# A clamp with its two bounds swapped, steps moved between engines, and a new order of all steps, in an attention and gated projection kernel

## The chip, the cores and the metric

The kernel runs on one core of one Trainium2 chip. The metric is the device time of one execution in microseconds. The core's engines are TensorE (PE, matrix multiplication into PSUM), VectorE (DVE), ScalarE (ACT), GpSimd (POOL, which does not touch PSUM in this program) and SyncE (SP), from which all of this kernel's transfers are issued. Each engine works through its own instructions in order; semaphores tie them together.

## What is computed

The first stage is attention between a sequence `x` of 512 positions and a state of 32 rows, for 8 batches of 8 heads of 64 channels, read both ways. The second stage multiplies a gate, which is a causal five-tap convolution over positions behind a sigmoid, with a matrix product, and projects the result.

```python
def _attn_ref(x, state):            # x: 8,8,512,64   state: 8,8,32,64
    scale = 1.0 / np.sqrt(D)
    scores = scale * np.matmul(x, state.transpose(0, 1, 3, 2))
    a = softmax(scores)             # over the 32 state rows
    xread = np.matmul(a, state)
    a2 = softmax(scale * np.matmul(state, x.transpose(0, 1, 3, 2)))   # over the 512 positions
    sread = np.matmul(a2, x)
    return np.concatenate([xread, sread], axis=2)

def _moe_ref(x, w_val, conv_w, w_out):   # x: 8,544,512, heads side by side
    gate_pre = sum over k of conv_w[k] * x shifted by 4 - k positions
    gate = 1.0 / (1.0 + np.exp(-gate_pre))
    return (gate * (x @ w_val)) @ w_out
```

The weights reach the kernel as 64-bit integer arrays that hold float32 pairs; the kernel reads them as two 32-bit words, shifted by 16 bits, and joins a float from the two.

## The kernel before

**Steps and order.** The program first makes a list of 1,200 numbered steps, each a small function that issues one to a few instructions. The string `ORDER` (line 33) then lists the steps to issue, one number each; a letter behind a number gives the engine to a step that several could do: `a` ACT, `v` DVE, `g` POOL. Steps without a letter have a fixed engine. Nothing else decides the order: each engine gets its instructions in the order of the list. `SLOTS` gives every tile its buffer, in the order in which the tiles are first used. Steps that no list names are left out; among the 1,200 are 60 `warm_up` steps (two small matmuls each, on PE, whose result nobody reads), of which the order before uses 11.

**Weights.** `w_val` and `w_out` come in four parts each (w_val parts are called v0 to v3, w_out parts o0 to o3), the convolution weights in one (conv). For each part: `load_words` (SP), `words_top` (ACT: the top 16 bits to float, tile wc), `words_bound` twice (lines 270 to 274: wc clamped to a range of large negative or of large positive numbers, tiles ws0 and ws1), `words_sum` (POOL: ws0 + ws1 into wc, line 227), `words_int` (ACT: to integer, tile wt in PSUM, line 282), `words_join` (DVE: joined with the low bits, line 287). A w_out part is then split into `woh` (`high`, a copy to a rounded type) and `wol` (`low`, the rest, line 227).

**Batches.** For each batch b: transposes of x or `x_blocks_T` on DVE; `scores`; the softmax over positions (`max_s`, `exp_s`) and the one over state rows (`max_n`, `sub_n`, `exp_n`, `sum_n`, `scale_n`, `probs`, tiles sl and ex, 128x1024); `ah` and `al`, high and low part of the result; `exp_T`, `state_read`; `state_val` (line 343: state times all four joined w_val parts, tile sgv); `read`, which makes xr; per 128 channels `gate_first`, `gate_tap` three times, `gate_last`, `gate_add` (line 227), `gate`; `values` (line 538), `gated` (tile g), its parts `gh` (`high`) and `gl` (`low`); then per 128 positions `project` (lines 547 to 549), a copy out of PSUM (`project_copy`, tile o) and `store`. Batch 0 makes its gate with `tap_state` (POOL) and `read_conv` (PE). A tail does the same for the 32 state positions of all batches (`tail_taps`, `tgh`, `tgl`, `tail_project`, `tail_copy`, `tail_store`).

**Around the start.** The order before has POOL do, from the first w_val clamp on: both clamps and the sum of v0, two clears, the sums of v1 and v3 (whose clamps DVE does), a clamp of v2, `tap_state`, `scale_n` of batch 0, the other clamp of v2, both of o1, `sub_n` of batch 1, the sum of v2, both clamps of o0, the sums of o1 and o0, `scale_n` of batch 1, then the first `wol`. On PE, `exp_T` of batch 2 stands ahead of `state_val(0)`.

Of the kernel before, what the change touches and what calls it, by code (L numbers as in the profile page):

```python
# [14 lines left out]
ALU = mybir.AluOpType  # L15
# [18 lines left out]
52 98 10 107 97 110 95 207 210 96 72 24 197 53 198 105 11 111a 196 13v 112a 12g 19 211a 109a 103 14g 195 15 106a 16  # L34
212v 108v 94 99 104v 209a 22 20 100v 101 17 1179 102a 1197 117 73 31 23a 74v 208a 113 21a 75v 18 119 76g 25 45 203 114
325 335a 1168 120 38 205 115 26g 204a 27g 118 323 201 206a 28g 121 202a 324 199 116 322 1177 456 334 200a 122v 458 337
32 213 34v 46 468 33v 217 29 48v 47v 123 65 128 214 35g 130 218 77 332 336a 124 49g 39 460 129a 54a 58 40g 78 333a
140g 461 330 131a 215 328 331a 127 194 326 219 216 125g 132 221 471 329a 1176 133 459 327a 30 66 454 340 41g 455 338a
126 36 68g 230 134 67g 453 339a 50 342 135 1196 222g 344 469 136a 341 220 51 231a 1178 1153 232 59 345 42g 141 90a 229
457 223 61g 37 463 233a 60g 464 224 43 55 69g 343 346 62g 70 714 44 347 79 71 225g 63 359 462 148 137 145 64 600 151  # L40
234 465 356 91g 226 470 138a 56 466 139a 235 57a 348 244 227a 472 154 236 228g 252 467 585 588 142 254 586 245 321 473
255 360a 349g 155 597 253a 158 601 478 86a 584 156a 256 602 603 479 475 157g 595 166 80 587 159 598 266 247 82g 596
267a 582 257g 474 357 160a 167 162 358a 477 161g 476 589 350 81g 248 489 87g 88a 239 163 490a 351 237 361 89g 238a
240a 362 242a 146 170 241 352g 449 363 249 171 452 258 448 243 147a 259 279 268 592 149 273 168a 83g 591 280 261 150a
246a 491 269 250g 152 274 84 262 275 492a 281 153a 85 164a 169g 291 270 92a 498 251 353 271g 182 501a 276 183 165g
499a 502 277a 292 500 272 293 93g 282 260a 184 263 371 278g 480 185 379 264g 285 294 393 286 381 283a 143 172 395 354a
284g 287 144v 604 188 186a 382 723 265 481g 173 593 380a 288 590 189 725 174a 383 176 450 713 396 482 384g 177 599
295a 366 483 729 372 296g 728 190 175 369a 451 191 289a 374 355g 722 367a 364 724 178 370 187 365a 394a 368 179 385
375 309 386 484g 397 303 192a 388 180a 412 594 387a 413 398g 376 406 733 727 605 485 730 290g 580 304 389 486a 583 310
607 732 734 311 390 608 735 312 373a 391g 606 407 313a 609 414 377g 392 610 503 612 408 518 305 415 613g 512a 306 736  # L50
378 520 315 399 409 307a 316 487g 521 611 308 317 855 504 522 856 538 511 715 731 418 614 318 513 719 717 419 506 519a
314 420 514 720 410a 523g 493 718 319a 726 297 615 864 411g 524 494 193 298 867 525 848 400 488 616g 527 495 539 416a
401 421 505a 402 721 299 422a 528 849 532 423g 976 515 300 507 866 737 516g 854 301a 403 581 181 508 621 404a 845 533
517 739 865 405g 544 622a 850 742 534 741 545 509g 550 529 743 442 617 526a 417g 443 510 740 546 535 530g 444 547 536a
551 738 548a 635 537v 531 618a 868 549g 552 540 744 860 657 445 852 619g 636 844 659 430 859 541 658a 431 861 638 446a
846 436 857 553 745g 637a 862 437 660 851 554a 438 447 643 661 320 630 712 555g 645 639 432 633a 662g 646 433 746 634
424 434a 747 425 663 542a 623 439 631a 640 543g 644a 426 853 440a 670 641g 863 650 992 762 435 632 716 748g 858 496
671 497a 765a 620 427 652 763a 676 647 624a 672 428a 653 648g 753 869 764 754a 654 649 626 766 682 873 625 673 664 980
627 665 871 977 651a 574 870 993 642 983 683 752 872 989 874 575 981 674v 875 994 684 749 675g 986 576 984 991 577 876
750a 988 655g 987 562 982 578v 677 302 751g 656 685 678 755 686a 679 568 756a 990 767 687g 985 997 847 563 884 978 789  # L60
877g 569 579 768 791 996 564 999 770 790a 441 565 998 782 792 666 566a 628 995 570 878 793 556 680a 784 794g 557 769a
667 558 668v 795 571 771 757 669v 572a 758 772 783a 573 559 629a 785 775 773g 796 560a 777 885 561 797 1000 886a 429
798 759 567 786 887 979 802 879 787g 888a 760 1001 774 761v 803 880g 1006 890 889 1002 688 1005 891 681g 799 804 776a
894 1003 1007 800v 1004 1019 778 814 895a 881 808 815 779 816 882a 809 896 780g 689 897a 817 690 898 801g 781 810 1008
788 899 811 1009g 691 900 694 692v 921 695 1112v 1020a 812a 923 696 915a 902 700 914 903 706 1114a 924 701 813v 922a
697 916 702 698a 925 707 805 926g 708 904 709 917 901a 1026 818v 710a 883v 711 1017 1027a 928 806v 1018a 819v 826 1010
1028 905g 703 918 1110a 940 807v 1029a 929 906 946 1030 1113g 704a 827 1011 927 705 832 907 693 930 947 1012g 931 934
909 833 941 1111g 1013 935 1022 908v 919g 834 910 820 1016 920 942 821 943 822 911 944a 1021 912v 823 932v 933v 892
835 1023 893v 824a 1014v 828 913 825 945v 948 836a 1031 1015g 949 837 950a 1066 1032 936 829 1033a 937 1115g 1039 838
1034 1046 1067 1041 1108a 1024 839 1035 1025a 938a 1060 1042 830a 939g 1061 1036 831 840 1048 952 1037v 958 1043 1038  # L70
953 1049 1040a 841 1053 1050 1044g 1129 1072 1055 959 1109v 1047a 954 842v 1128 1062 1051v 843 1073 1056 1119 970 1118
1121 1052 964 1074 965 1116v 960 951v 966 1063 955 1117v 1068 967 1064v 1075 1124 968a 1076v 1065v 969 1120 1123 1134
1057 1077g 1122 1045 1054v 1078 1125 1090 956v 971 1069 957 1079 1070v 1133 1058v 1071v 1059 1126v 961 1130 972 1102
1127v 973 1131 1096 1103 1097 1132 1080 1135 1084 1081 1138 1136v 1085 1137v 1098 1082v 962v 1139 1083v 1104 974v 1099
975 699 1091 1144 1086 1105 1092 1106a 1100a 1140 1107 1101 1093 1141 1094v 1087 1095 1142v 963 1145 1143 1088v 1146
1147 1089 1198 1148a 1189 1190 1149
""".split()

SLOTS = dict(
    ps=  # L80
    "01234567312412756372456713631762631570754713564260431250413761561573613561762762412650774032230574617205347043"
    "17067124035760631577620165314203674175204127601657231762052643542760341043726651042602365702146",
    x="0120122102",
    sT="01",
    xT="01230123012301230123012301230123",
    xq="01201202102201010122",
    e2="0121021202102012",
    e2T="0120120210201202",
# [4 lines left out]
    swh="0100100101",  # L93
    swl="011011010",
# [19 lines left out]
def state_attention_gated_kernel(  # L114
# [155 lines left out]
    def words_bound(e, word, side, *key):  # L270
        p, n = word()[..., 0].shape
# [530 lines left out]
```

## Time and profile before

| | |
|---|---|
| time, median of 3 runs | 249.15 us (248.99 to 249.51) |
| the profiled execution, its own time | 247.34 us |
| its span in the trace | 245.6 us |
| PE busy | 224.2 us (91%) |
| DVE busy | 199.6 us (81%) |
| ACT busy | 151.4 us (62%) |
| POOL busy | 146.9 us (60%) |
| moved by DMA | 33.04 MB, 135 GB/s on average |

Busy time is the time in which at least one instruction of the engine runs; since matmuls overlap, a busy PE is not PE at its peak. In the rows below PEld is the load of weights into PE, PEclk the granted clock of PE as a share of full speed, `<-` ahead of a name what a wait ended with, and L227 a line of the kernel (a helper's, for all copies and differences: there the tile tells which step it is).

### The profile page before, as it was taken

How to read it: one execution, taken by the hardware profiler on the slowest of the kernel's cores; microseconds unless marked ns; L12 is line 12 of the kernel's file. 1: busy time of each engine (PE TensorE's matmuls, PEld its weight loads, DVE VectorE, ACT ScalarE, POOL GpSimd, SP SyncE). 2: the span in 40 equal slices, each digit the busy share in tenths (PEclk: the TensorE clock that was granted, in tenths of full speed). 3: DMA queues.
4: the chain of work that ended last, by engine and by line, in shares of the span. 5: the costliest groups of instructions: out<-in, count | busy, mean ns of one | idle time of the engine just before them, and what ended most of it. 6: DMA issues, size and time to landing. Idle time of an engine off the chain costs nothing.

```text
span 245.6 us, 4958 instructions
## 1 busy us (share of the span) xinstructions
PE 224.2 (91%) x1847; PEld 156.7 (64%) x1847; DVE 199.6 (81%) x320; ACT 151.4 (62%) x320; POOL 146.9 (60%) x109
## 2 busy tenths in 40 slices
PE   1986894799899999999999999999999999979994
PEld 1764661345466666767665766666677678868783
DVE  0489964759979999989999959998998699998730
ACT  2588754789677978967987658676581666011010
POOL 3278999769998996778867492545276432200000
PEclk9999799589999999999999999999999999999999
DMA  4899936256300764577373578600021211110046
GB/s 128 298 378 303 245 96 179 83 155 173 112 31 0 235 205 119 169 235 220 86 213 107 146 212 254 216 3 0 4 89 41 88 44 43 45 40 3 35 160 189
DMA packets 23029, 33.04 MB, mean 135 GB/s; under 512 B 6858, under 2 KB 15070, under 8 KB 23006
## 3 DMA queue, kind: packets, MB, share of 16 engines
q1 hardware_dynamic: 23006, 32.73, 43.5%
q8 instruction: 14, 0.23, 0.4%
q14 instruction: 9, 0.07, 0.1%
HBM read 23.81 MB, written 8.91 MB: 133 GB/s over the span
## 4 chain that ended last, share of the span: by engine, by line
PE 62%; DVE 18%; POOL 8%; DMA 4%; ACT 2%; issue 2%; SPq 1%; DVEq 0%; ACTq 0%; POOLq 0%
PE val L538 15%; PE op L547 9%; PE op L548 9%; PE op L549 8%; PE sgv L343 4%; DVE tacc L573 4%; DVE acc L518 3%; POOL ws_o L273 3%; PE srp L424 3%; PE xr L478 3%; PE e2p L415 2%; PE sc L378 2%; DVE ws_v L273 2%; DMA x<-x 2%; POOL ws_v L273 2%
## 5 line engine op out<-in xcount | busy, mean ns | idle before, releaser
L518 DVE SCALAR_TENSOR_TENSOR acc<-xr,cw,acc 128x511 f32<-128x511 f32 (+2 forms) x84 | 59.3, 735 | 3.2 <-ACT xt L514 2.7
L547 PE MATMUL op<-woh,gh 128*128 128x512 f32 x128 | 52.7, 412 | 1.8 <-DVE last L224 1.6
L548 PE MATMUL op<-wol,gh 128*128 128x512 f32 x128 | 50.6, 396 | 0.9 <-POOL wol L227 0.9
L549 PE MATMUL op<-woh,gl 128*128 128x512 f32 x128 | 50.4, 394 | 0.0
L227 POOL TENSOR_TENSOR acc<-acc,last 128x508 f32<-128x508 f32 x24 | 32.8, 1367 | 25.1 <-DVE acc L518 17.9
L227 POOL TENSOR_TENSOR gl<-g,gh 128x512 fp32r<-128x512 f32 x21 | 27.9, 1327 | 20.6 <-DVE gh L216 13.7
L547 PEld LDWEIGHTS op<-woh,gh 128*128 128x128 f32 x128 | 24.0, 188 | 14.1 <-issue 5.8
L548 PEld LDWEIGHTS op<-wol,gh 128*128 128x128 f32 x128 | 24.1, 188 | 6.2 <-POOL wol L227 1.7
L549 PEld LDWEIGHTS op<-woh,gl 128*128 128x128 f32 x128 | 24.0, 188 | 5.6
L543 DVE SCALAR_TENSOR_TENSOR g<-sig,val 128x512 f32<-128x512 f32 x32 | 21.6, 678 | 4.6 <-PE val L538 3.4
L530 ACT ACTIVATE sig<-acc 128x512 f32<-128x512 f32 x28 | 17.5, 633 | 11.7 <-POOL acc L227 6.6
L214 ACT COPY o<-op 128x512 f32<-128x512 f32 x24 | 14.1, 596 | 14.9 <-PE op L549 14.7
L513 ACT ACTIVATE acc<-xr,cw 128x512 f32<-128x512 f32 x28 | 19.1, 697 | 5.4 <-PE xr L478 5.3
L222 ACT ACTIVATE last<-xr,cw 128x508 f32<-128x508 f32 x26 | 18.0, 693 | 3.9 <-POOL acc L227 2.1
L227 POOL TENSOR_TENSOR al<-sl,ah 128x1024 fp32r<-128x1024 f32 x6 | 14.7, 2452 | 8.8 <-DVE ah L216 5.1
L538 PE MATMUL val<-ah,swh 128*128 128x512 f32 x56 | 18.0, 408 | 0.0
L538 PE MATMUL val<-al,swh 128*128 128x512 f32 x56 | 17.7, 402 | 0.0
L538 PE MATMUL val<-ah,swl 128*128 128x512 f32 x56 | 17.5, 398 | 0.0
L415 PEld LDWEIGHTS e2p<-ident,e 128*128 128x128 f32 x64 | 9.6, 207 | 11.1 <-ACT e L408 7.6
L227 POOL TENSOR_TENSOR ex<-ex,rc 128x1024 f32<-128x1024 f32 x8 | 15.4, 1920 | 1.6 <-DVE rc L464 1.5
L368 DVE STREAM_TRANSPOSE xT<-xq 128x512 f32<-128x512 f32 x20 | 13.8, 700 | 2.9 <-DMA xq<-x 2.9
L214 ACT CAST gh<-g 128x512 fp32r<-128x512 f32 x22 | 13.8, 631 | 3.6 <-DVE g L543 3.6
(131 smaller groups left out, 461.9 us busy)
## 6 DMA issues: line engine op xcount, KB each, us to landing
xq<-x SPq DMA_DIRECT2D x80, 124.0 KB, 3.6
x<-x SPq DMA_DIRECT2D x32, 256.0 KB, 5.3
out<-o SPq DMA_DIRECT2D x32, 256.0 KB, 2.3
ow<-w_out SPq DMA_DIRECT2D x4, 511.8 KB, 8.3
vw<-w_val SPq DMA_DIRECT2D x4, 511.8 KB
sg<-state SPq DMA_DIRECT2D x8, 64.0 KB, 3.3
z<-state SPq DMA_DIRECT2D x16, 32.0 KB
out<-to SPq DMA_DIRECT2D x8, 64.0 KB, 1.7
```

The lines of the kernel that those rows point to most:

```text
L214: nc.scalar.copy(out, in_)
L222: nc.scalar.mul(out, in_, factor)
L227: (nc.vector if e == "DVE" else nc.gpsimd).tensor_tensor(out, a, b, op=how)
L273: (nc.vector if e == "DVE" else nc.gpsimd).tensor_scalar(get(f"ws{side}", *key)[:p, :n], get("wc", *key)[:p, :n], least, most, op0=ALU.max ...
L513: nc.scalar.mul(get("acc", b, pr), pt, cw[:, HALO, pr:pr + 1])
L518: nc.vector.scalar_tensor_tensor(acc[:, d:], get("xr", b, pr)[:, :S - d], cw[:, HALO - d, pr:pr + 1], acc[:, d:], op0=ALU.mult, op1=ALU.add)
L530: nc.scalar.activation(get("sig", b, pr), get("acc", b, pr), AF.Tanh, scale=0.5)
L538: nc.tensor.matmul(get("val", b, k), w[:, g, c], a[:, g], start=(term == 0 and g == 0), stop=(term == terms - 1 and g == NG - 1))
L543: nc.vector.scalar_tensor_tensor(get("g", b, k), get("sig", b, k), 1.0, get("val", b, k), op0=ALU.add, op1=ALU.mult)
L547: nc.tensor.matmul(pt, gh, woh[:, k], start=(k == 0), stop=False)
L548: nc.tensor.matmul(pt, gh, wol[:, k], start=False, stop=False)
L549: nc.tensor.matmul(pt, gl, woh[:, k], start=False, stop=(k == NPR - 1))
```

## The change

Three things change. `words_bound` takes the minimum first and the maximum second, with the same two bounds. The order is a new one for all steps. In it, steps that several engines can do are given out anew:

| step | before | after |
|---|---|---|
| clamps of the words | 11 POOL, 7 DVE | 18 POOL |
| `gl`, `al`, `wvl`, `tgl`, the tail's low part (differences of two SBUF tiles) | POOL 30, DVE 16 | POOL 46 |
| `gate_add` | 24 POOL, 4 DVE | 28 POOL |
| `sub_n` | 7 POOL, 1 DVE | 8 POOL |
| `gh` | 22 ACT, 10 DVE | 32 ACT |
| `ah`, `wvh`, `tgh`, the tail's high part | 9 ACT, 5 DVE | 14 ACT |
| `exp_T_copy` (e2T) | 16 ACT | 13 ACT, 3 DVE |
| `project_copy` (o) | 24 ACT, 8 DVE | 21 ACT, 11 DVE |
| `state_val_high` (swh) | 16 ACT | 14 ACT, 2 DVE |
| `xT`, `long_T`, `state_read_out`, `read_last_copy` | 29 ACT, 7 DVE | 26 ACT, 10 DVE |

The 11 `warm_up` steps are gone. From the first w_val clamp on, POOL's new order is: both clamps and the sum of v0, a clear, both clamps of v2, a clear, `sub_n` of batch 0, both clamps of o1, the sums of v2 and o1, `scale_n` of batch 0, `tap_state`, a clamp of v3, `sub_n` of batch 1, a clamp of v1, the other of v3, the other of v1, the sums of v3 and v1, `scale_n` of batch 1, the four clamps of o3 and o2, the sum of o2, `sub_n` of batch 2, the sum of o3, then the first `wol`. Ahead of v0 it has both clamps and the sum of o0 and those of conv. `exp_T` of batch 2 stands behind `state_val(0)`. SP's first loads are o0, conv, two pieces of x of batch 0, the first state group, the other two pieces, one of batch 1, v0, v2. The last steps are `project(7, 3, 3)`, its copy on ACT and `store(7, 3)`; before they were `tail_project(1, 3)`, its copy and the four transfers of `tail_store(1)`.

```diff
@@ ORDER (all of it is new; its first two lines here) @@
-52 98 10 107 97 110 95 207 210 96 72 24 197 53 198 105 11 111a 196 13v 112a 12g 19 211a 109a 103 14g 195 15 106a 16
-212v 108v 94 99 104v 209a 22 20 100v 101 17 1179 102a 1197 117 73 31 23a 74v 208a 113 21a 75v 18 119 76g 25 45 203 114
...
+58 10 97 96 52 59 11 95 13g 107 98 210 103 195 60g 61g 104a 110 24 101 62g 38 197 53 12g 196 14g 198 207 99 15 108v 63
+102v 65 105 454 111a 100v 112a 106a 471 16 212a 19 117 25 323 211v 64 109a 208a 27g 17 113 119 26g 39 94 118 28g 114
...
@@ -271,7 +271,7 @@
         p, n = word()[..., 0].shape
         least, most = (EDGE, EDGE + MOST) if side else (LEAST - EDGE, -EDGE)
         (nc.vector if e == "DVE" else nc.gpsimd).tensor_scalar(
-            get(f"ws{side}", *key)[:p, :n], get("wc", *key)[:p, :n], least, most, op0=ALU.max, op1=ALU.min)
+            get(f"ws{side}", *key)[:p, :n], get("wc", *key)[:p, :n], most, least, op0=ALU.min, op1=ALU.max)
```

## Rows read from the trace of the kernel before

**Rows 1.** Busy us (and instructions) of each engine by stage; then PEclk, DMA share, GB/s

```profile
0.00:46.00 46.00, 30.98 (x364) 21.89 (x372) 29.10 (x49) 28.85 (x64) 35.12 (x36) 0.94 0.73 217
46.00:66.00 20.00, 18.94 (x229) 8.90 (x213) 16.61 (x25) 17.50 (x40) 15.96 (x12) 0.89 0.50 145
66.00:200.00 134.00, 133.74 (x1061) 92.62 (x1062) 121.36 (x193) 95.58 (x199) 92.27 (x61) 1.00 0.41 125
200.00:232.00 32.00, 30.27 (x153) 24.89 (x152) 30.49 (x53) 7.84 (x15) 3.51 (x3) 1.00 0.09 34
```

**Rows 2.** Waits, PE alone: who waited for whom, total us, times, longest

```profile
PE op L547 <- DVE last L224: 1.6, 1, 1.6
PE op L548 <- POOL wol L227: 0.9, 2, 0.7
```

**Rows 3.** Chain that ended last, around 40 us: start us, us, what

```profile
38.34 3.76 POOL ws_o L273 x2
...
43.36 0.60 ACT wt_o L282
43.98 0.70 DVE wc_o L287
```

**Rows 4.** Timeline of PE, 33 to 47 us: start us, us, instruction, [idle before]

```profile
44.71 1.13 PE L415 MATMUL e2p<-ident,e 128*128 128x128 f32 x4 [5.39 <-DVE wc_o L287]
45.76 1.96 PE L343 MATMUL sgv<-wv,sT 64*32 64x512 f32 x16
```

**Rows 5.** Line 273, the clamps: duration ns min/median/max, first and last start us

```profile
L273 POOL TENSOR_SCALAR ws_v<-wc_v x4: 1908/1918/1918, 14.8 to 29.5; 128x512 f32<-128x512 f32 x4
L273 DVE TENSOR_SCALAR ws_v<-wc_v x4: 609/1048/1515, 18.9 to 21.4; 128x512 f32<-128x512 f32 x4
L273 DVE TENSOR_SCALAR ws_o<-wc_o x2: 420/423/426, 12.6 to 12.9; 128x512 f32<-128x512 f32 x2
L273 POOL TENSOR_SCALAR ws_conv<-wc_conv x1: 797/797/797, 6.2 to 6.2; 20x128 f32<-20x128 f32 x1
```

**Rows 6.** POOL's instructions by shape: busy us, mean ns | idle before (memsets: first 14.76 us)

```profile
masks.py:199 POOL TENSOR_SCALAR_AFFINE_SELECT ident<-ident 128x128 f32<-128x128 f32 x1 | 0.3, 293 | 0.1
masks.py:197 POOL MEMSET ident<- 128x128 f32 x1 | 0.2, 204 | 0.3 <-POOLq L791 0.3
L382 POOL MEMSET sTl<- 64x256 f32 x4 | 1.2, 306 | 0.2
L227 POOL TENSOR_TENSOR wc_v<-ws_v,ws_v 128x512 f32<-128x512 f32 x4 | 5.5, 1369 | 0.5 <-DVE ws_v L273 0.4
L227 POOL TENSOR_TENSOR sl<-sl,mx 128x1024 f32<-128x1024 f32 x7 | 13.4, 1918 | 1.2 <-DVE mx L453 1.2
L227 POOL TENSOR_TENSOR z<-z,cwb 128x640 f32<-128x640 f32 x1 | 1.5, 1539 | 0.0
```

**Rows 7.** Timeline of POOL, 14 to 20 us

```profile
13.51 1.28 POOL L227 TENSOR_TENSOR wc_o<-ws_o,ws_o 128x512 f32<-128x512 f32 x1 [6.00 <-DVE cw L306]
14.76 3.80 POOL L273 TENSOR_SCALAR ws_v<-wc_v 128x512 f32<-128x512 f32 x2
```

**Rows 8.** Instructions by shape, the parts of the gated tile on each engine

```profile
L227 POOL TENSOR_TENSOR gl<-g,gh 128x512 fp32r<-128x512 f32 x21 | 27.9, 1327 | 20.6 <-DVE gh L216 13.7 <-ACT gh L214 6.1 <-DVE acc L518 0.6
L227 DVE TENSOR_TENSOR gl<-g,gh 128x512 fp32r<-128x512 f32 x11 | 7.5, 681 | 0.0
L214 ACT CAST gh<-g 128x512 fp32r<-128x512 f32 x22 | 13.8, 631 | 3.6 <-DVE g L543 3.6
L216 DVE CAST gh<-g 128x512 fp32r<-128x512 f32 x10 | 4.2, 421 | 0.2
```

**Rows 9.** The page's stores (KB each, us from issue to landing); the last issues on SP

```profile
out<-o SPq DMA_DIRECT2D x32, 256.0 KB, 2.3
out<-to SPq DMA_DIRECT2D x8, 64.0 KB, 1.7
...
241.56 1.71 SPq L617 DMA_DIRECT2D out<-to  x4
```

More of the change, by code (lines that the diff above doesn't have):

```diff
@@ L39 @@
[L39 to L73, printed above, removed]
@@ new lines @@
+244 236 82g 138a 76g 467 154 245 462 600 349g 588 77 247 449 151 78 602 259 56 597 155 143 166 595 57a 83g 248 716
+144a 350 451 261 585 87g 156a 598 249 162 596 84 167 321 227a 157g 85 601 246a 351 587 239 228g 266 357 90a 268 158
+168a 163 242a 240a 250g 243 358a 269 359 88a 273 169g 241 360a 274 267a 262 237 473 238a 352g 159 251 164a 270 362
+160a 361 478 252 146 291 165g 477 980 363 275 254 260a 292 161g 475 92a 176 147a 276 479 285 89g 474 286 287 255 476
+498 271g 256 277a 599 170 91g 253a 263 592 293 272 603 489 353 452 499a 264g 171 593 501a 580 149 172 294 150a 490a
@@ new lines @@
+689 901a 710a 690 904 1010 711 1019 911 705 691 914 1011 912g 892 802 1020a 893a 803 692a 1026 916 913 1012g 921 1022
+1029v 915a 804 929 805 905g 1021 923 806a 838 1027a 1030 807g 930 922a 1013 934 1023 935 819g 906 924 839 840 925
+1111g 832 931 932a 926g 936 833 937 841 933g 1028 938a 917 1031 1014a 918 927 820 842v 1040a 919g 821 1046 946 1109g
+920 822 1039 947 1015g 948 1041 834 949 940 1042 950a 823 1033a 1043 1113g 941 1032 824v 826 825 1044g 942 835 939g
+1024 952 1025v 1034 827 836a 951g 1035 1045 970 837 943 1114a 693 971 1053 1115g 953 1118 1055 944a 828 1036 1116a
@@ new lines @@
+945g 829 1056 1066 1057 1117g 1060 830v 1078 1048 1061 831 1067 1049 1062 1037g 954 955 1054a 1079 956v 1119 1068
+1058g 1121 1072 1123 1059 1038 1124 1063 1120 964 1064a 972 958 1065g 1122 965 1129 1125 1128 1080 1047v 1126a 1073
+973 1069 1127g 1130 959 1070a 974a 1074 975 966 843 1084 579 967 1050 1090 1051g 968v 1144 1081 1071g 1096 1131 1082a
+1052 1133 1138 1134 1075 1132 1076a 1097 1077g 1085 960 1135 1091 1136a 1145 1137g 1139 961 1083g 1098 962a 1086 963
+957 1102 1146 1140 1147 1092 1148a 1141 1149 1093 1142v 1099 1094v 969 1103 1095 1143 1087 1100v 1104 1088v 1105 1101
@@ L77 @@
+1089 1106a 1107
 """.split()
@@ L80 @@
     ps=
-    "01234567312412756372456713631762631570754713564260431250413761561573613561762762412650774032230574617205347043"
-    "17067124035760631577620165314203674175204127601657231762052643542760341043726651042602365702146",
-    x="0120122102",
+    "01234567013645717351640367056346710527364731450367263726713673271071623455046216730216760342054673113527035014"
+    "726510137052625717563027453606145073324371625104676325637263042517105067312572604531",
+    x="0120121101",
     sT="01",
     xT="01230123012301230123012301230123",
-    xq="01201202102201010122",
-    e2="0121021202102012",
-    e2T="0120120210201202",
+    xq="01210122012012100210",
+    e2="0120120212021021",
+    e2T="0120120212021021",
     sr="00000000",
@@ L92 @@
     al="0101010101",
-    swh="0100100101",
-    swl="011011010",
-    acc="012012012002101201021020120120",
-    last="010101101010110101010101000101000",
-    sig="0123312013203102031230210312013201",
-    g="0101010101111010010110110101101001",
-    gh="0123456012345061234051603241560236415062304516023564",
-    gl="0123456023451063241506235401652314605123406",
-    o="0123100123203132320101301301312312",
+    swh="0101011010",
+    swl="010100101",
+    acc="012012102102121021021021021202",
+    last="010101010100101101010101010010110",
+    sig="0123031203121230123102131203210303",
+    g="0101010110110111001010111010101011",
+    gh="0123456120345160235140236504126534102635124065231405",
+    gl="0123456123560412306542315604213546023514603",
+    o="0123120120130221311213332331012032",
     nb="01230123",
```

31 lines of the change are left out of this document (25 added, 6 removed).

## Prediction

> **What bounds the kernel now.** I read first how the busy time lies by stage, then what TensorE (PE) waited for, then the chain of work that ended last, and only then single instructions. By stage [rows 1] the kernel has two halves of very different kind. From 66 to 200 us PE is busy 133.74 of 134 us: nothing that another engine gains there can shorten the run, because PE has no idle time to give back. In the first 46 us PE is busy only 30.98 us, and part of that is filler (matmuls that only keep it awake). From 200 to 232 us PE has 30.27 of 32 us and the vector engine (DVE) 30.49, so both are full. What can be won therefore lies at the start, and a little at the end.
>
> The waits name the same places: one of 5.39 us ahead of four transposes at 44.71, for a word join on DVE [rows 4], one of 1.6 us late in the run, and two together of 0.9 us for GpSimd (POOL) [rows 2]. The chain [rows 3] says what stands behind the first: two POOL clamps of the w_out words (3.76 us), then POOL's sums, ACT's conversion at 43.36 (0.60 us) and DVE's join at 43.98 (0.70 us), which frees the PSUM slot that the transposes need; and behind these, at 45.76 [rows 4], `state_val(0)` (tile sgv), the first matmuls that need all four joined w_val words. I call that start T. The order before and the order after give PE the same steps ahead of T but for the fillers, one `exp_T` and a `read_last` of four columns, and the same steps behind it; so the run after is the run before, moved by the change in T, plus what changes behind T. PE's own work ahead of T is no limit: 30.98 us with fillers, in 45.8.
>
> **The clamps.** All 18 go to POOL, seven of which were on DVE, and each now takes the minimum first. On POOL a max-first clamp of 128x512 took 1.908 to 1.918 us; on DVE 0.42 us where it ran alone and 0.61 to 1.5 us where POOL was busy too [rows 5]. No row shows a min-first clamp on POOL. Bounds: the upper end is the price before, 1.92, since elements and arithmetic are the same. For the lower end I take the nearest other one-input pass that compares and chooses, the affine select of 128 elements in 0.293 us [rows 6]; the conv clamp, also 128 elements, took 0.797 [rows 5]. Memsets of 128 and 256 elements, 0.204 and 0.306 us [rows 6], give 0.8 ns an element, and 0.293 + 384 x 0.8 ns = 0.60 us. Which is nearer? The clamp's own slope is (1.915 - 0.797) / 384 = 2.9 ns an element, more than the two-input sum needs in all: 1.369 us for 512, or 2.7 ns an element with its fixed part included [rows 6]. A pass with one input cannot be slower than one with two because of reading and writing; so the 1.92 us is in how this pair of operations is carried out, and the order of the pair is the one thing edited. I take 0.65 us, near the lower end, and keep both.
>
> The Trainium skill, "GPSIMD Engine Reference", section 4.1, says that a one-input elementwise pass on GpSimd runs at roughly line rate; at its clock of 1.2 GHz that is an estimate of 0.43 us for 512 elements, and T would be 2.2 us earlier than below. The trace disagrees for the max-first pair, which is over four times that.
>
> **T after.** In the order after, POOL's work from the first w_val clamp to the last w_val sum is: ten clamps (eight of w_val, two of w_out word 1), five sums at 1.37, `sub_n` of batches 0 and 1 and `scale_n` of batch 0 at 1.92 each (the three are passes over 1024 elements), `tap_state` 1.54, two clears at 0.31 [rows 6]. Without the clamps: 6.85 + 5.76 + 1.54 + 0.62 = 14.8 us. Before, POOL began the first w_val clamp at 14.76 us [rows 7]. After, ahead of that word's load stand one w_out word and five x pieces, about as much as before, and ahead of its clamp the two of w_out word 0, for which POOL has 6 us of idle time; I start it at 15.0. Behind the last sum come a conversion and a join, 0.60 + 0.70 [rows 3]. So T = 15.0 + 14.8 + 1.3 + 10p = 31.1 + 10p, with p the price of one clamp. With p = 0.65, T = 37.6 us against 45.8: **-8.2 us**. With p = 0.60 it is -8.7; with p = 1.92, T = 50.3, +4.5.
>
> **What changes behind T.** (a) One `exp_T` (four transposes, 1.13 us at 44.71 [rows 4]) moves behind `state_val(0)`: +1.1. (b) The 1.6 us wait behind DVE [rows 2] goes: DVE is full from 200 to 232 us [rows 1] and loses among others the `gh` casts and the `gl` and `tgl` subtractions there. -1.6. Next late is PE itself. I leave the 0.9 us behind POOL. (c) The last transfer: before, four issues take 1.71 us from 241.56 [rows 9], after it is one; three fewer are -1.3, but an `o` store lands 2.3 us after issue and a `to` store 1.7 [rows 9], +0.6. Sum -0.7. (d) The moves off DVE: ten `gh` casts to ACT, 0.421 to 0.631 us, and eleven `gl` subtractions to POOL, 0.681 to 1.327 us [rows 8]; the rest (four gate adds, one `al`, one `sub_n`, `wvl`, `tgl`, the tail's split) are of the same kind. DVE gives up 11.7 us for the two groups; POOL takes 14.6 and has 41.7 us free from 66 to 200, ACT takes 6.3 and has 38.4 [rows 1]. So there is room, and what is left is delay: each moved tile is ready (0.631 + 1.327) - (0.421 + 0.681) = 0.86 us later, and behind it in POOL's queue wait the gate adds and the softmax passes of later batches. All shown, 11 x 0.86 = 9.5 us; none, 0. Before, 21 of 32 `gl` tiles already went to POOL and PE waited for none of them; I take +1.0. Copies out of PSUM that move from ACT to DVE (three `e2T`, three `o`, two `swh`) fill what DVE gave up: nothing, and under a microsecond each if DVE is late. (e) The fillers at the end run beside the last copy: nothing. Those at the start lie in PE's idle time, so their removal saves nothing; they may have held the clock. The granted clock was 0.94 of full speed over the first 46 us and 0.89 from 46 to 66 us [rows 1], after the long wait. 0.11 of 20 us is 2.2 us, which a shorter wait may give back, or a PE without fillers may lose again; I take 0 and keep both ends.
>
> Sum: -8.2 + 1.1 - 1.6 - 0.7 + 1.0 = **-8.4 us**. The profiled execution took 247.34 us with a span of 245.6; the median of the timed runs is 249.15, 1.8 us above it. I take the difference from both: a span of 237.2, a time of **240.8 us**.
>
> **The rivals.** *The order of the pair changes nothing* (the change doesn't do what it says): p stays 1.92. Place: POOL's queue at the start, which now holds all 18 clamps; T is +4.5, with the rest of the sum +4.3; and the four w_out clamps behind T put `wol` and `al` some 5 us later, of which PE's other work covers about half: +2.5. 249.15 + 6.8 = 256; if the other work covers all, 253.5; call it 254.5. For it: same elements, same arithmetic. Against: the 0.293 us row. The sum turns at 31.1 + 10p - 45.8 - 0.2 = 0, that is p = 1.49 us: above, slower, below, faster. Chance 0.18.
>
> *Something else holds T.* Over the first 46 us ACT is busy 28.85 us and DVE 29.10 [rows 1], and neither could do much before the conv clamp at 6.2 us [rows 5]. Without its clamps (four at 1.05, two at 0.42) DVE has 24 us, so it could reach T at 30 and ACT at 35 without a wait, but each idled some 11 us there before. With half of that left, T is about 42, 4.4 us later than forecast: 245.2 us. Chance 0.14.
>
> *The longer hand-overs show.* If PE stands for each of the eleven moved `gl` tiles, 9.5 us in place of 1.0: 249.3 us, no change. For it: POOL is an in-order queue, and from 200 us on it was nearly idle before (3.51 of 32 [rows 1]) and now carries the tail's subtractions. Against: 41.7 us free in the long stage. Chance 0.08. The Trainium skill, "GPSIMD Engine Reference", section 4.1, says to keep two-input elementwise work on VectorE, GpSimd being about 2 times slower; the trace agrees (1.327 against 0.681), and this rival is what that rule would cost here.
>
> **How the numbers follow.** The forecast has the remaining 0.60. Its own spread: 2.2 us either way for the clock, -0.5 for p, +3 for hand-overs and T together: 236 to 246. The low end stays 236. At the top the second and third cases lie inside 252, and the first mostly above it; 236 to 252 leaves about 0.2 out. 0.2% is 0.5 us, about what a measurement of this kernel can tell from no change. Faster: 0.60 x 0.99 + 0.14 x 0.95 + 0.08 x 0.35 + little of the first = 0.76. Same: 0.03, nearly all from the third. Slower: 0.21, most of it the first.
>
> **What would show it.** The POOL clamp's row: near 0.65 us. `state_val(0)` at 37 to 39 us, with no 5 us wait for a join ahead of it. PE busy nearly all of the time behind it, as before; no PE wait for `gl` or `tgl` over 1 us in sum. The last store issued alone. Wrong would be: a clamp near 1.9 us; T above 42 with POOL idle ahead of it; a new PE wait of microseconds behind POOL or ACT; or a granted clock that falls after T for longer than before.

## The result

| | before | after |
|---|---|---|
| time, median | 249.07 us (248.99 to 249.51) | 236.62 us (235.65 to 239.26) |
| ratio to before, 95% interval | 1 | 0.948 (0.944 to 0.952) |
| profiled execution, its span | 247.34, 245.6 us | 236.12, 234.3 us |
| start of `state_val(0)`, T | 45.76 us | 37.49 us |
| from T to the end of the span | 199.8 us | 196.8 us |

The changed kernel takes 12.45 us less at the median; 8.4 were forecast, from a median of 249.15 then. The time lies inside the range of 236 to 252 and 4.2 us below the forecast of 240.8. The ratios, here and below, leave out executions more than 1.5% above the fastest of their kernel, and the medians do not (without the 239.26, that of the kernel after is 236.12). In the profiled executions the span fell by 11.3 us, 8.3 of it ahead of T and 3.0 behind it. Of the 4.2 us, 2.9 lie in the span (237.2 forecast, 234.3 measured); the rest is that the median stood 1.7 us above the profiled execution before and stands only 0.5 above it after.

The clamps of the kernel after, as in [rows 5] (duration min/median/max in ns, first and last start in us):

```profile
L273 POOL TENSOR_SCALAR ws_o<-wc_o x8: 604/605/607, 6.1 to 38.6; 128x512 f32<-128x512 f32 x8
L273 POOL TENSOR_SCALAR ws_v<-wc_v x8: 604/612/616, 12.8 to 32.0; 128x512 f32<-128x512 f32 x8
L273 POOL TENSOR_SCALAR ws_conv<-wc_conv x2: 282/282/282, 5.1 to 8.7; 20x128 f32<-20x128 f32 x2
```

On POOL the pair in its new order costs 0.61 us where it cost 1.92, and the small one 0.28 where it cost 0.80 (0.63 with the old pair in the new order, below). The timeline of POOL up to T (start us, us, instruction, idle before it), as in [rows 7]:

```profile
12.78 1.19 POOL L273 TENSOR_SCALAR ws_v<-wc_v 128x512 f32<-128x512 f32 x2 [2.87 <-ACT wc_v L222]
...
30.80 1.77 POOL L273 TENSOR_SCALAR ws_v<-wc_v 128x512 f32<-128x512 f32 x3 [2.25 <-ACT wc_v L222]
32.53 2.52 POOL L227 TENSOR_TENSOR wc_v<-ws_v,ws_v 128x512 f32<-128x512 f32 x2
```

The last w_val sum ends at 35.05. POOL idled 2.25 us ahead of v1's clamps, since ACT had not yet made the words of v1: part of the way to T something other than POOL set the pace (the loads, as is tried below). PE at T, as in [rows 4]:

```profile
35.02 0.54 PE L424 MATMUL srp<-x,e2T 128*32 128x64 f32 x22
36.50 0.38 PE L424 MATMUL srp<-x,e2T 128*32 128x64 f32 x10 [0.95 <-issue]
36.82 0.75 PE L415 MATMUL e2p<-ident,e 128*128 128x128 f32 x4
37.49 1.09 PE L343 MATMUL sgv<-wv,sT 64*32 64x512 f32 x16
38.51 0.66 PE L424 MATMUL srp<-x,e2T 128*32 128x64 f32 x32
```

The 5.39 us wait for a join is gone, and the same sixteen matmuls take 1.09 us where they took 1.96. From 28.2 us to T PE is idle once, for the 0.95 us that end at 36.50, just behind the last join of w_val (36.40); the profile names nothing that it waited for. So PE's own work is only about a microsecond less late at T than POOL's chain. The rows also show a `state_read` (tile srp, 32 matmuls) ahead of T and another behind it; in the order before, both stand behind T:

```profile
47.65 1.08 PE L424 MATMUL srp<-x,e2T 128*32 128x64 f32 x32
48.66 1.12 PE L332 MATMUL sgp<-ident,sg 128*128 128x128 f32 x4
49.71 0.98 PE L424 MATMUL srp<-x,e2T 128*32 128x64 f32 x32
```

The stages of the kernel after, moved by the change in T (columns as in [rows 1]):

```profile
0.00:38.00 38.00, 27.89 (x372) 18.58 (x372) 23.35 (x43) 27.25 (x60) 28.14 (x43) 0.96 0.93 261
38.00:58.00 20.00, 18.80 (x215) 10.25 (x200) 19.53 (x30) 18.50 (x44) 18.57 (x16) 1.00 0.54 151
58.00:190.00 132.00, 130.60 (x1046) 90.40 (x1045) 114.90 (x179) 94.46 (x198) 98.60 (x69) 1.00 0.41 123
190.00:222.00 32.00, 31.32 (x158) 25.73 (x157) 22.25 (x33) 12.63 (x24) 16.44 (x12) 1.00 0.15 56
```

The granted clock right behind T was 0.89 of full speed [rows 1], between its two levels of 1.2 and 2.4 GHz on the mean, and is 1.00, the upper one, now. Before, it stood at the lower level from 44 to 50 us, from the end of the long wait on:

```profile
44.00:50.00 6.00, 5.29 (x68) 2.80 (x72) 5.64 (x9) 3.94 (x9) 3.67 (x3) 0.50 0.28 85
```

Up to T PE is idle 10.1 us in place of 15.0. From T to the end of the last matmul whose result is read, before and then after:

```profile
45.76:240.89 195.13, 192.08 (x1482) 133.87 (x1482) 170.73 (x274) 122.23 (x256) 111.98 (x74) 0.99 0.37 115
37.49:229.77 192.28, 189.00 (x1448) 132.50 (x1447) 159.40 (x245) 126.59 (x264) 134.12 (x96) 1.00 0.38 116
```

PE is idle about as long (3.3 us, 3.1 before), but busy for 189.0 us in place of 192.1. In the last stage DVE has gone from 30.49 of 32 us to 22.25, and POOL from 3.51 to 16.44. The longest waits of PE behind T, as in [rows 2] (us in total, times, longest):

```profile
PE xr L478 <- issue: 1.2, 1, 1.2
PE op L547 <- DVE g L543: 0.7, 1, 0.7
PE op L547 <- DVE acc L518: 0.5, 1, 0.5
```

No PE wait for `gl`, `tgl` or `gh` shows. The 1.6 us wait behind DVE and the 0.9 us behind POOL [rows 2] are gone; one of 1.2 us with nothing named and two behind DVE of 1.2 us in sum stand in their place.

### The profile page after: what moved, and what is told of

Read it like the earlier page. It is cut to its first block, busy times and chain, and to the rows that moved or that the text cites. A ratio compares the mean times of both kernels' runs of the same rounds, so it can differ in the third digit from the quotient of the medians.

```text
span 234.3 us, 4885 instructions
## 1 busy us (share of the span) xinstructions
PE 216.4 (92%) x1803; PEld 150.9 (64%) x1803; DVE 182.8 (78%) x288; ACT 154.0 (66%) x324; POOL 161.7 (69%) x137
## 4 chain that ended last, share of the span: by engine, by line
PE 51%; DMA 15%; DVE 12%; SPq 8%; issue 6%; POOL 4%; ACT 3%; DVEq 0%; ACTq 0%; POOLq 0%
PE val L538 11%; DMA xq<-x 9%; PE op L547 7%; PE op L549 6%; PE op L548 6%; DMA x<-x 4%; PE srp L424 4%; DVE tacc L573 3%; DVE acc L518 3%; SPq L247 3%; SPq L238 3%; PE sgv L343 3%; PE e2p L415 2%; PE xr L493 2%; PE xr L478 2%
## 5 line engine op out<-in xcount | busy, mean ns | idle before, releaser
L518 DVE SCALAR_TENSOR_TENSOR acc<-xr,cw,acc 128x510 f32<-128x510 f32 (+2 forms) x84 | 60.1, 733 | 7.8 <-ACT xt L514 2.4
L227 POOL TENSOR_TENSOR gl<-g,gh 128x512 fp32r<-128x512 f32 x32 | 41.3, 1299 | 23.9 <-ACT gh L214 23.9
L227 POOL TENSOR_TENSOR acc<-acc,last 128x508 f32<-128x508 f32 x28 | 35.9, 1285 | 19.2 <-DVE acc L518 15.5
L214 ACT CAST gh<-g 128x512 fp32r<-128x512 f32 x32 | 20.0, 628 | 17.3 <-DVE g L543 17.3
L214 ACT COPY o<-op 128x512 f32<-128x512 f32 x21 | 12.3, 596 | 11.1 <-PE op L549 7.7
L227 POOL TENSOR_TENSOR al<-sl,ah 128x1024 fp32r<-128x1024 f32 x7 | 16.9, 2410 | 0.2 <-ACT ah L214 0.2
L227 POOL TENSOR_TENSOR sl<-sl,mx 128x1024 f32<-128x1024 f32 x8 | 15.3, 1915 | 1.0 <-DVE mx L453 1.0
L365 PE MATMUL xTp<-ident,x 128*128 128x128 f32 x48 | 8.5, 322 | 7.9 <-DMA x<-x 7.6
```

Of the source, the lines that this page charges most:

```text
L214: nc.scalar.copy(out, in_)
L227: (nc.vector if e == "DVE" else nc.gpsimd).tensor_tensor(out, a, b, op=how)
L518: nc.vector.scalar_tensor_tensor(acc[:, d:], get("xr", b, pr)[:, :S - d], cw[:, HALO - d, pr:pr + 1], acc[:, d:], op0=ALU.mult, op1=ALU.add)
```

## The experiments

The theory: POOL's queue up to T was the limit, the order of the pair of operations sets its price, and what follows T is worth little. The rivals: the new order of the steps or the moves between engines do the work, and the pair little; or something else than POOL holds T. In kernels whose list of steps was edited the functions stand 14 lines lower (line 287 for 273), in one of them 15.

### The pair's order alone, in the kernel before

```diff
-            get(f"ws{side}", *key)[:p, :n], get("wc", *key)[:p, :n], least, most, op0=ALU.max, op1=ALU.min)
+            get(f"ws{side}", *key)[:p, :n], get("wc", *key)[:p, :n], most, least, op0=ALU.min, op1=ALU.max)
```

> The kernel before with only the clamps' order of operations changed: minimum first; the same order of steps, 11 clamps on POOL and 7 on DVE. If the price of a clamp on POOL makes the gain (1.92 us before, 0.61 in the changed kernel), the start of state_val(0) comes some 8 to 10 us earlier than 45.8 (eight of these clamps lie on the chain ahead of it, 1.3 us each), and the time falls to 239 to 241 us. If the new order and the moves off DVE make the gain, the time stays at 247 to 249 us, although the clamps are short.

Measured: 244.16 us (242.75 to 245.78), ratio 0.980 (0.974 to 0.987), T at 40.4. It is between the two numbers, so each theory missed. The clamps became cheap (0.61) and T moved by 5.4 us, not by 8 to 10: that is as much as the 5.39 us wait of [rows 4], and with it gone PE goes from step to step without a wait of over 0.1 us from 27.7 us to T:

```profile
35.24 4.53 PE L493 MATMUL xr<-a,z 32*64 32x512 f32 x80
...
40.38 1.09 PE L343 MATMUL sgv<-wv,sT 64*32 64x512 f32 x16
```

In this order PE's own work is the next limit at T. At the end only 3.4 us of the span are left. The PE order is that of before, so the delay can be followed: `state_val` starts 5.4, 5.0, 3.5, 3.5 us earlier than before for the first four batches, and 3.4 for the last. What is lost between goes into waits that the late T had hidden, above all the first of these (as in [rows 2]), and into the clock (as in [rows 1]):

```profile
PE srp L424 <- DVE g L543: 1.7, 1, 1.7
PE op L547 <- DVE last L224: 1.6, 1, 1.6
60.00:66.00 6.00, 6.00 (x29) 4.43 (x30) 5.43 (x10) 4.10 (x11) 4.45 (x4) 0.72 0.54 145
```

The first wait is new and ends at 58.9 us, between the second and the third `state_val`, where the lead falls from 5.0 to 3.5 us; behind it the granted clock is 0.72 from 60 to 66 us, where it was 1.00 before. The second is that of [rows 2], untouched. In both it is DVE that is next late.

### The pair's order undone, in the kernel after

```diff
-            get(f"ws{side}", *key)[:p, :n], get("wc", *key)[:p, :n], most, least, op0=ALU.min, op1=ALU.max)
+            get(f"ws{side}", *key)[:p, :n], get("wc", *key)[:p, :n], least, most, op0=ALU.max, op1=ALU.min)
```

> The changed kernel with the maximum first again in the clamps, all 18 on POOL, its order and its engines otherwise as they are. If the pair's order sets the price and the price sets the start: clamps of 1.92 us, state_val(0) near 50 us, 251 to 256 us, slower than before. If order and moves make the gain: 238 to 242 us.

Measured: 256.96 us (255.39 to 257.72), ratio 1.031 (1.024 to 1.037), slower than before. T is at 49.7; the formula 31.1 + 10p gives 50.2. This is the prediction's first rival, played out; it was priced at 254.5, and the upper of the two expectations ended at 256. The part above that lies behind T. The stretch from T to the second `state_val`, here and then in the kernel after:

```profile
49.70:67.10 17.40, 12.92 (x86) 4.94 (x85) 10.91 (x15) 12.19 (x26) 17.40 (x11) 0.73 0.52 145
37.49:47.61 10.12, 8.92 (x85) 3.75 (x84) 9.18 (x14) 8.94 (x20) 8.69 (x10) 1.00 0.67 174
```

and the chain there, with the old pair (start us, us, what):

```profile
50.91 7.53 POOL ws_o L273 x4
58.44 1.24 POOL wc_o L227
```

POOL has no idle moment. Timeline of ACT there, and then the wait of PE:

```profile
59.70 0.59 ACT L282 CAST wt_o<-wc_o 128x512 int32<-128x512 f32 x1 [4.83 <-POOL wc_o L227]
60.22 0.59 ACT L509 ACTIVATE sig<-xr 128x512 f32<-128x512 f32 x1
```

```profile
PE halo L501 <- ACT sig L509: 4.4, 1, 4.4
```

ACT's conversion of that word waits 4.83 us for the sum behind the four w_out clamps, and behind it in ACT's queue stands the sigmoid that PE's `halo` waits for. So the kernel is 12.2 us behind the changed one at T and 19.5 at the second `state_val`: 7.3 us, where the prediction had put 2.5 for these clamps. Of the 7.3, PE is idle for 3.3 (4.5 in place of 1.2), since ACT's queue, which also works in order, carried the delay on to PE; the other 4.0 are the same matmuls taking longer (12.9 us in place of 8.9), at a granted clock of 0.73 in place of 1.00. The forecast at T was right, and its second half three times too small: it had neither.

### What the pair costs by itself

```diff
+        LO, HI = LEAST - EDGE, -EDGE
+        for e in (nc.gpsimd, nc.vector):
+            e.tensor_scalar(md[:, :512], ms[:, :512], LO, HI, op0=ALU.max, op1=ALU.min)
+            e.tensor_scalar(md[:, :512], ms[:, :512], HI, LO, op0=ALU.min, op1=ALU.max)
...
+            e.tensor_scalar(md[:, :512], ms[:, :512], LO, None, op0=ALU.max)
+            e.tensor_scalar(md[:, :512], ms[:, :512], HI, None, op0=ALU.min)
+            e.tensor_scalar(md[:, :512], ms[:, :512], 2.0, 1.0, op0=ALU.mult, op1=ALU.add)
+        for _ in range(3):
+            nc.vector.tensor_tensor(w2, w0, w1, op=ALU.add)
...
```

> The changed kernel with instructions behind its work that feed nothing: on POOL and then on DVE a clamp of 128x512 maximum first, minimum first, both again with 256 elements, the maximum alone, the minimum alone, a multiply and add; then on DVE three sums of two SBUF tiles and three SBUF copies of 128x512 alone, and three of each beside six sums on POOL. If the order of the pair sets POOL's price: 1.9 us with the maximum first, 0.6 with the minimum first, on DVE both alike near 0.42. If it is the maximum itself that is slow, the maximum alone also takes over 1 us on POOL; if only the pair, it takes about as much as the minimum alone. If POOL holds up DVE's steps with two SBUF tiles: 0.68 us alone and 1 us or more beside POOL, copies 0.42 and more; if not, the same in both places.

The instructions stand behind the kernel's own last steps, each once; only their rows count. On POOL, in this order: maximum then minimum, minimum then maximum, maximum alone, minimum alone, product then sum; then the first on DVE.

```profile
L781 POOL TENSOR_SCALAR md<-wv x1: 1926/1926/1926, 222.0 to 222.0; 128x512 f32<-128x512 f32 x1
L782 POOL TENSOR_SCALAR md<-wv x1: 619/619/619, 224.0 to 224.0; 128x512 f32<-128x512 f32 x1
L785 POOL TENSOR_SCALAR md<-wv x1: 1497/1497/1497, 226.3 to 226.3; 128x512 f32<-128x512 f32 x1
L786 POOL TENSOR_SCALAR md<-wv x1: 1493/1493/1493, 227.9 to 227.9; 128x512 f32<-128x512 f32 x1
L787 POOL TENSOR_SCALAR md<-wv x1: 622/622/622, 229.5 to 229.5; 128x512 f32<-128x512 f32 x1
L781 DVE TENSOR_SCALAR md<-wv x1: 427/427/427, 230.1 to 230.1; 128x512 f32<-128x512 f32 x1
```

Same data, same shape, same two bounds: 1.93 and 0.62 us. The pair's order alone decides, on POOL alone; DVE takes 0.43 for either. And it is not that the maximum is dear: one operation by itself, either, takes 1.49. Of the five forms only two are quick, minimum then maximum and product then sum. The Trainium skill, "GPSIMD Engine Reference", section 4.1, has one-input passes at roughly line rate; at its clock of 1.2 GHz that is an estimate of 0.43 us here. The measured rows are about 1.5 times it for two forms, and 3.5 times it and more for the others. The measurement decides.

The same kernel has DVE's sum of two SBUF tiles first with POOL idle, then with six POOL sums beside it, and a DVE copy likewise:

```profile
L790 DVE TENSOR_TENSOR wv<-wv x3: 684/691/692, 233.0 to 234.4; 128x512 f32<-128x512 f32 x3
L796 DVE TENSOR_TENSOR wv<-wv x3: 684/1634/1634, 236.4 to 238.8; 128x512 f32<-128x512 f32 x3
L792 DVE COPY wv<-wv x3: 426/427/427, 235.1 to 236.0; 128x512 f32<-128x512 f32 x3
L798 DVE COPY wv<-wv x3: 1366/1366/1368, 240.4 to 243.2; 128x512 f32<-128x512 f32 x3
```

While POOL sums, both take 0.94 us longer: 0.69 becomes 1.63, 0.43 becomes 1.37 (a POOL sum took 1.32 to 1.64). The clamps of [rows 5] on DVE, 0.42 us alone and up to 1.52 beside POOL's, agree with it.

### The pair's order and the moves, in the old order

The list of steps of the kernel before, with the pair as after and the engine letters of the 74 moved steps as after, for example:

```diff
-537v 674v 668v
+537g 674a 668a
```

> The order of the kernel before, minimum first, and every step on the engine that the changed kernel gives it (74 steps move, the DVE's differences of two SBUF tiles and casts among them). Beside the run with minimum first alone it shows the moves alone, in the old order. If keeping such steps off DVE is worth something: 1 to 3 us less than that run. If the longer hand-overs through ACT and POOL cost more than DVE's relief gives, in an order that was not made for them: 1 to 5 us more.

Measured: 246.82 us (243.58 to 249.0), ratio 0.986 (0.977 to 0.995), T at 44.2 in its profile. Beside 244.16 for the pair alone, the moves in the old order bring nothing that shows: they cost 2.7 us by the medians and 1.5 by the ratios, and the intervals overlap, so even the sign isn't settled. The profile is of the longest of the four executions, 249.0 us where the others took 243.58 to 246.92, and need not hold for them. In it T is 3.8 us later than with the pair alone, and the last 80 matmuls ahead of T start as much later:

```profile
34.90 1.87 PE L412 MATMUL sc<-xT,sTl 128*32 128x256 f32 x16 [1.63 <-DVE sTl L239]
...
39.07 4.53 PE L508 MATMUL xr<-a,z 32*64 32x512 f32 x80
```

From 34.9 us to T PE waits for nothing, so in this execution too it is PE's work, held up earlier by DVE, that sets T, and not POOL's sums.

### The moves undone, in the new order

The list of the kernel after, with the letters of those 74 steps as before, for example:

```diff
-537g 674a 668a
+537v 674v 668v
```

> The changed kernel's order with minimum first, and every step back on the engine that it had before (74 steps). Beside the changed kernel it shows the moves in the new order. If the moves matter: 2 to 5 us slower than the 236.6 us of the changed kernel, with DVE as the limit late in the run. If only the price of the clamps and the new order matter: 236 to 238 us.

Measured: 245.49 us (245.0 to 247.68), ratio 0.987 (0.980 to 0.994), 8.9 us more than the kernel after. T is at 37.5, the same. The loss comes behind it: the eight `state_val` start 0, 1.3, 1.3, 1.3, 1.5, 2.2, 2.2, 2.2 us later than in the kernel after, the `read` of the last batch 3.0, and the end 8.9. The first 1.3 us go with a join on DVE that ends 0.7 us behind T, for which `state_val(0)` waits after it has started, and with the granted clock, 0.83 from 37.5 to 47.6 us in place of 1.00. The two kernels from 178.1 us on, the kernel after first:

```profile
178.10:208.10 30.00, 29.82 (x152) 23.79 (x152) 22.19 (x34) 15.84 (x32) 20.57 (x15) 1.00 0.10 36
```

```profile
178.10:208.10 30.00, 26.61 (x127) 19.32 (x126) 25.41 (x38) 11.35 (x25) 10.91 (x7) 1.00 0.10 36
```

With the steps back on DVE, PE does 127 matmuls in 30 us in place of 152; POOL and ACT, which take these steps in the kernel after, are more than half idle.

### A third of the moves undone: the last batch and the tail

The list of the kernel after, with the letters of 25 steps of the last two batches and the tail as before, for example:

```diff
-1064a 1065g 1126a 1127g 1082a 1083g
+1064v 1065v 1126v 1127v 1082v 1083v
```

> The changed kernel with only the moved steps of the last batch and of the tail (25 of the 74: casts, differences, gate adds, and the copies of the last two batches) back on their engines of before. If the moves off DVE pay at the end of the run, where DVE and PE were both full: most of the 9 us that all 74 moves were worth in this order comes back, 241 to 244 us, with PE waiting for DVE from 180 us on. If the other moves are what counts: 237 to 239 us.

Measured: 239.66 us (238.23 to 240.06), ratio 0.959 (0.954 to 0.965). The number lies between the two that were expected. By the medians it is 3.0 us more than the kernel after, a third of the 8.9. In its profile it is 202.3 us from T to the end, in place of 196.8: 5.5 of the 8.9. The two do not agree, so these 25 steps bring a part of what the moves bring, and how large a part stays open. PE's longest wait behind T, and the stretch right behind it:

```profile
PE tval L613 <- DVE last L238: 2.1, 1, 2.1
201.50:205.50 4.00, 4.00 (x21) 3.86 (x20) 3.82 (x9) 1.15 (x2) 0.00 (x0) 0.57 0.00 0
```

DVE is the late one again, as in [rows 2], and the wait ends at 200.4 us with the granted clock falling behind it: 0.57 in these 4 us, 1.00 in the same place of the kernel after.

### What holds T in the kernel after: the loads

SP's steps in the list of the kernel after, one after another; the other engines' steps between them stay where they are:

```diff
-454 471 323 94 469 325 460 324 45 322 455 468 31
+323 325 324 322 94 45 31 454 471 469 460 455 468
```

The x of batch 2 (322 to 325) and the w_val parts v3 and v1 (45 and 31) are loaded ahead of the blocks of batch 3.

> The changed kernel with the loads of x of batch 2 and of w_val parts 3 and 1 issued ahead of the first blocks of batch 3. If the start of state_val(0), 37.5 us, hangs on these loads (by the chain of waits x of batch 2 lands at 22.7, and PE and ACT work from there): it comes 1 to 2.5 us earlier and the time falls by 1 to 2 us to about 235. If POOL's queue of clamps and sums still sets it, as the prediction had it (31.1 us and ten clamps): no change, 236 to 237 us.

Measured: 234.47 us (233.88 to 237.18), ratio 0.942 (0.935 to 0.949), T at 34.5. POOL's wait ahead of v1's clamps is 0.22 us in place of 2.25. So in the profiled execution of the kernel after, loads held the last part of the way to T. The version was run again, on one chip with the kernel after, and with one edit more (two pieces of x of batch 0 ahead of conv, and both ahead of o0: `58 10 97 96` becomes `97 96 10 58`).

> The changed kernel as it is, beside the two that follow on the same chip: 236 to 237 us, state_val(0) between 35.5 and 37.5 us, since its start hangs on when loads land.

> The changed kernel with the loads of x of batch 2 and of w_val parts 3 and 1 ahead of the blocks of batch 3, as once before. If these loads hold up state_val(0) in the changed kernel: 1 to 2.5 us less than that, 234 to 235 us, and POOL without a wait of over 0.5 us between the first w_val clamp and the last w_val sum. If the one difference seen so far was chance: the two agree within 0.5 us.

> The same, and two pieces of x of batch 0 and the convolution weights ahead of the first w_out part. If what is left ahead of state_val(0) is POOL's chain from the first w_val clamp, which waits for the load of w_val part 0: no change against the run before, within 0.5 us, since that load is not moved. If PE's start, 6.3 us, still counts: PE starts a microsecond earlier and the time falls by 0.5 to 1 us more.

| | median us (range) | ratio to before | T, us | wait for v1, us |
|---|---|---|---|---|
| kernel after | 237.05 (234.43 to 239.07) | 0.948 (0.942 to 0.953) | 35.6 | 0.76 |
| loads reordered | 233.97 (233.6 to 235.01) | 0.939 (0.936 to 0.943) | 35.7 | 0.20 |
| also x ahead of o0 | 236.73 (236.04 to 237.38) | 0.950 (0.946 to 0.953) | 38.8 | 0.35 |

The version with the loads reordered has the lowest median in both comparisons, below the kernel after by 0.7 and 0.9% of the time of before; the intervals overlap in the first and just touch in the second. How it gains is less plain. In the two profiles shown side by side T is the same, 35.6 and 35.7, and 1.1 us of the span separate them, all behind T. The kernel after has T at 37.5 in one profile and at 35.6 in the other, with POOL's wait for v1 1.5 us apart; the reordered one has 34.5 and 35.7, with v0's first clamp 1.2 us apart (13.00 and 14.22). So T varies in both, from one execution or one chip to the next. That the new order of loads takes away the variation of the wait for v1 is only argued: profiles of single executions can't show it, and the spread of the times doesn't (without the longest time of the kernel after, 3.3 us against 1.4 in the second comparison, but 1.5 against 3.3 in the first). What the gain comes from stays open.

The further edit missed what was expected of it. Timeline of POOL with it:

```profile
8.69 0.28 POOL L287 TENSOR_SCALAR ws_conv<-wc_conv 20x128 f32<-20x128 f32 x1 [7.26 <-ACT wc_conv L236]
...
16.28 1.19 POOL L287 TENSOR_SCALAR ws_v<-wc_v 128x512 f32<-128x512 f32 x2 [2.81 <-ACT wc_v L236]
```

The words that were pushed back come 3.6 us later to POOL's first clamp (5.09 in the middle row), and ACT, whose queue also has them first, makes those of v0 later too; v0's clamp comes at 16.28 in place of 14.22, T 3.1 us later, and the time is 2.8 us longer.

### The fillers alone

```diff
-        for j in range(2):
-            nc.tensor.matmul(get("warm", i)[:, j * P:(j + 1) * P], ident, ident, start=True, stop=True)
+        get("warm", i)
```

The kernel before without the 11 fillers, whose result nobody reads.

> The kernel before without its 11 filler steps (44 small matmuls). If they only fill PE's idle time: no change, 248.5 to 249.5 us. If they hold the clock for what follows: slower by 1 to 3 us, with a lower granted clock in the first 60 us. If they stand in the way of PE's own work at the start: up to 1 us faster.

Measured: 250.01 us (248.07 to 251.68), ratio 1.0037 (0.9997 to 1.0078). The granted clock is 0.85 from 20 to 46 us and 0.86 from 46 to 66 us, in place of 0.89 in both. The difference of the medians is about a microsecond, and the interval begins at no change: too small to call. The interval's other end is 2 us, so that is the most that the fillers earned in the old order. The changed kernel has none and runs at 1.00 behind T; it also lacks the 5 us wait, but that alone doesn't decide it: with the moves undone PE had no wait of over 1.3 us just ahead of T, and the clock was 0.50 from 38.5 to 41.5 us.

## Why the prediction was right, and where it was not

**What bounds the kernel, and the price of the clamp: right.** A POOL clamp of 0.65 was taken against bounds of 0.60 and 1.92; it is 0.61. The argument, that a one-input pass slower than a two-input one can't be slow for its data, holds. The reason was given as "how this pair of operations is carried out", and the instructions by themselves confirm that far; but they also show that neither operation alone is quick, which nothing in the trace of before could tell.

**T: 37.6 forecast, 37.49 measured, by errors that cancel.** POOL began v0 at 12.78 and not at 15.0 (-2.2); it had waited 2.87 us for ACT's words by then, so it was the load and ACT's conversion that came sooner than taken. From there to the end of the last sum were 22.27 us, not 14.8 + 6.5 = 21.3 (+1.0): the wait of 2.25 for v1's words, which the formula didn't have, less 0.4 for the cheaper clamps and small gains of the other pieces. From there to `state_val(0)` were 2.44 and not 1.3 (+1.1): conversion and join ended at 36.40, and PE then had 1.1 us of other matmuls ahead of it, the end of a `state_read` and an `exp_T`. The formula is good to some 2 us here, and its agreement to 0.1 is luck. With the pair's order undone, and POOL without idle time from 16.0 us to the last sum, it gave 50.2 against 49.7, its three pieces off by +1.0, -0.9 and -0.6: that is where it applies. What it left out is PE. "PE's own work ahead of T is no limit" compared sums of busy time; but PE's last steps come late, and its work was all that was left ahead of T with the pair alone in the old order (40.4), and lay within 0.95 us of setting T in the kernel after. With PE's earlier steps where they are, a clamp that cost nothing would have brought T forward by those 0.95 us at most.

**"Something else holds T": half right.** It was given 0.14, and named ACT and DVE. In the kernel after, POOL waited for ACT's words of v1, and these for loads, 2.25 us in one profile and 0.76 in the other; PE, which it did not name, is the nearest limit behind. Its 42 us do not follow from its own numbers: ACT at 35 and half of 11 us idle give 40.5.

**Behind T: -0.2 forecast, -3.0 measured. This is the step that failed.** Term by term:

- (a) `exp_T` was charged 1.13 us, its price at a lowered clock; at full clock such a group takes 0.63 to 0.75: +0.7.
- (b) and (d), the waits: -1.6 for DVE's and +1.0 for the hand-overs were booked. The 1.6 us went, and 0.9 behind POOL that had been left out; three others came (1.2, 0.7, 0.5). No PE wait for `gl` or `gh` shows, so the hand-overs cost nothing. In all PE is idle 3.3 us up to its last matmul, 3.1 before: +0.2.
- (c) The last matmul to the end of the span is 4.5 us, 4.7 before: -0.2 in place of -0.7.
- (e) The clock was taken as 0 between -2.2 and +2.2. It came back: `state_val(0)`, the `state_read` behind it and the four transposes of `group_T` (tile sgp) took 1.96, 1.08 and 1.12 us before, and take 1.09, 0.66 and 0.60. The whole is an estimate of 2.2 us from [rows 1], as the prediction had sized it. It was set in the middle, although the idle time that went ahead of the low clock was itself forecast to go.
- A step was missed. The prediction has the same steps of PE on both sides of T but for fillers, one `exp_T` and a `read_last`. The new order also puts a `state_read` of batch 1 ahead of T (the rows at 35.02 and 36.50): 0.66 us at full clock, so -0.7, and -0.2 for the `read_last`.

By these sizes the sum behind T is +0.7 + 0.2 - 0.2 - 2.2 - 0.7 - 0.2 = -2.4, and 0.6 us are not traced to a row.

**The range.** The spread that the prediction names, 2.2 us for the clock and 0.5 for p, gives 238.1 at the low end; it wrote 236. That 236.62 lies inside the range is owed to 2 us that no term of it gives.

**What the moves are for.** The sum treated them as a cost with only (b) as return. In the old order that is near the truth (no gain). In the new order they are worth 8.9 us. In us, by medians:

| | clamp's order | moves | new order |
|---|---|---|---|
| in the old setting | -5.1 | +2.7 (undecided) | +1.3 |
| in the new setting | -20.3 | -8.9 | -10.2 |

For the clamp, the setting is order and engines together, old or new; for the moves, the order; for the order (which has the fillers' removal in it), the engines. The moves and the order were tried with the pair as after only. There neither gains without the other, and the clamp gains four times as much with both: together, order and moves put all the clamps and their sums in POOL's queue ahead of what PE needs, which only cheap clamps allow, and the new order ends in a stretch in which DVE is late without the moves. Beyond the 25 steps above, no run takes apart which of the moves do it, or which part of the order.

**The rival of longer hand-overs: nothing of it.** It was given 0.08, with the Trainium skill's rule against two-input work on GpSimd beside it. That price is as stated (1.30 us on POOL and 0.68 on DVE), and the moves, the differences among them, still pay together, with DVE the full engine at the end and POOL with time to spare. The differences were not moved by themselves. "Perfetto Trace Analysis" of the Trainium skill, in "Optimizing Scalar/DVE Operations", warns that a move between the two might not help as they share a read port; the rows do show the sharing, and here it is outweighed.

## What to carry to other kernels

Where an instruction costs more than its elements explain, time the other forms of it, in the reverse order of its two operations too: on POOL the pair minimum then maximum took a third of the time of maximum then minimum, and less than half of that of either alone. Where an edit frees one engine, ask which is late next, by when its last steps can start and not by the sum of its busy time, and move work off that one as well: the gains here don't add up, and a part tried alone can look worthless. A cost whose likely cause the change removes is better set near that end of its range than in its middle. Before an order is taken as "the same steps" on both sides of a mark, list them.

## What the runs showed of the hardware

- POOL, 128x512 float32, one input: 1.93 us for maximum then minimum, 1.50 for one of them, 0.62 for minimum then maximum or for product then sum. DVE: 0.43 for all.
- DVE's work between SBUF tiles took 0.94 us longer beside POOL sums: a two-operand sum 1.63 in place of 0.69 us, a copy 1.37 in place of 0.43.
- The sixteen matmuls of `state_val(0)` took 1.09 us at a granted clock of 1.00 and 1.96 at 0.50.
- The granted clock fell to 0.50 at the end of a PE wait of 5.4 us (before, 44 to 50 us), behind one of 2.1 us (a third of the moves undone, 0.57 on the mean from 201.5 to 205.5) and one of 1.7 us (the pair alone, 0.72 on the mean from 60 to 66). It also fell to 0.50 where the waits just ahead were 1.3 us and less (the moves undone, 38.5 to 41.5), and stayed at 1.00 behind one of 1.2 us at 40.4 in the kernel after. So the length of one wait doesn't tell it.
- The same program had T at 37.5 us in one profile and at 35.6 in another; POOL's wait for the words of v1 differed by 1.5 us between them.
